# One task and one PSUM bank for each head's scores, and a finer end, in a kernel of attention and a gated mixer

## The chip, the cores and the metric

The kernel runs on one core of a Trainium2 chip. The metric is the device time of one execution in microseconds, lower is better. "Profile" and "trace" mean one execution taken by the hardware profiler; its lines give engine, source line (L1601 is line 1601 of the kernel), operation and shapes.

## The reference

Two branches work on the same normalised input of 2048 rows and 640 columns. Branch A is attention with 32 heads of 20 columns, branch B a mixer that shifts columns along the sequence and a two-layer MLP. The output is x + A * silu(B).

```python
def _A_ref(x, wqkv, wo):          # B, S, D = 1, 2048, 640; H = 32; Dh = 20
    q, k, v = ...                 # from x @ wqkv, per head
    scores = jnp.einsum("bhqd,bhkd->bhqk", q, k) * (Dh ** -0.5)
    p = _softmax(scores, axis=-1)
    o = jnp.einsum("bhqk,bhkd->bhqd", p, v)
    return (...o as rows...) @ wo

def _B_ref(x, w1, w2, w3, w4):
    h = _gelu(_layernorm(x, axis=-1) @ w1)
    # four column groups of h, shifted by +1, -1, +2, -2 rows
    hs = jnp.concatenate([g0, g1, g2, g3], axis=-1) @ w2
    x1 = x + hs
    return x1 + _gelu(_layernorm(x1, axis=-1) @ w3) @ w4

xn = _layernorm(x, axis=-1)
return x + _A_ref(xn, A_wqkv, A_wo) * _silu(_B_ref(xn, B_w1, B_w2, B_w3, B_w4))
```

## The kernel before

The work of attention is cut into 8 quads of four heads (`attn_quad`, L1356), each into four chunks of 512 queries, and each chunk into 16 tiles of 128 keys. For a key tile, TensorE makes scores of 128 keys by 512 queries for each of the four heads; then the exponentials are taken, and TensorE multiplies them by the values and sums over the 16 key tiles in PSUM bank 7 (L1414, L1592).

One head's scores of a key tile fill one PSUM bank (512 float32 in each partition). Banks 0 to 6 are a pool from which all products take their space. The kernel works on scores two heads at a time: a *pair* is heads 0 and 1 (a = 0) or heads 2 and 3 (a = 1) of one key tile, and it lies in two banks side by side. An exponential covers such a pair, 128 x 1024 elements. Most are taken by ScalarE (`exp_act`, L1658, the ACTIVATE of L1663). For the key tiles that `order` marks as blocks (`score_both`, L1669), one of the two pairs goes to VectorE instead, which makes the exponent's bits as 16-bit integers in U (L1694); VectorE and GpSimd then add constants (L1580, L1578), and four products with the values follow (L1592). Thirteen key tiles are "wide": all four heads in four banks and one ScalarE instruction (`score_rows`, L1629; L1645).

Scores come in two forms. In the *row form* (L1601) a head's 32 partitions of keys and queries use one strip of 32 rows of the array, and the four heads' strips can work side by side. In the *column form* (L1616) the query matrix QM holds zeros for the other heads, all 128 rows are used, and a head takes four matmuls that lie side by side in strips of 32 columns. Everything else on TensorE uses strips of columns: the helper `mm_tile` (products at L715: projections, the mixer, the output projection) and the products with the values.

`score_pair` (L1603) is the task that makes one pair: it gets its two banks together (`acq=("S", hs)`), waits until both are free, issues two row matmuls (or eight column matmuls), and increments TensorE's semaphore after the last. `AGAIN` in the configuration names pairs that are computed twice, ten of them in quad 7.

Nothing loops on the device. The program builds a list of tasks with their reads and writes; `TABLE`, a long string at the end of the file, gives the order in which they are taken, with the banks that each gets. `Planner.follow` (L219) reads it, works out which scores take the row form (a task marked `flex` does so if it stands next to another one of scores), and `plan_sync` (L323) puts a semaphore wait ahead of a task for each task of another engine that it needs and that isn't known to be done. Each engine then runs its own list strictly in that order. A task marked `lock` is one on VectorE that isn't to meet GpSimd's work.

The end of the kernel is the last chunk (quad 7, chunk 3), cut in two halves of 256 queries (`last_half`, L1426). A half is normalised by four VectorE steps: transpose (L1545), reciprocal (L1547), multiply (L1552), transpose (L1554). Then follow, for each of its two output tiles of 128 rows, the product with the last quad's rows of wo (`wo_last`, L1831; matmuls L1840), a VectorE instruction that reads the product from PSUM and multiplies by the gate (L1847), and in `finish_qc` (L1866) an addition (L1890) and the store (L1892). Stores of even and odd tiles have a semaphore each (`stream=f"out{sl}"`), and a store waits until the one before it of the same name has landed.

Of the kernel before, what the change touches and what calls it, by code (L numbers as in the profile page):

```python
# [57 lines left out]
class Planner:  # L58
# [89 lines left out]
    def task(self, eng, dur, fn, reads=(), writes=(), due=None, name="", lat=0.0,  # L148
# [8 lines left out]
        t.part = part or 3 * mode  # L157
# [61 lines left out]
    def follow(self, table):  # L219
# [26 lines left out]
        while at < len(table):  # L246
# [11 lines left out]
            if e == "pe" and pe_mode and t.mode:  # L258
                st = max(row_at + 6.0, *(row_end[x] for x in (1, 2) if t.part & x))
# [27 lines left out]
            if e == "pe":  # L287
                if t.mode != pe_mode:
                    t.finish += self.mode_cost
                if t.mode:  # L290
                    row_at = t.finish - t.dur
                    if not pe_mode:
                        row_end[1] = row_end[2] = 0.0
                    for x in (1, 2):
                        if t.part & x:
                            row_end[x] = t.finish
# [168 lines left out]
class Handle:  # L465
    _n = 0

    def __init__(self):
        Handle._n += 1
        self.id = Handle._n  # L470
        self.slot = None


class Cfg:
# [5 lines left out]
    def __init__(self, S=2048, D=640, H=32, F=1536):  # L480
# [100 lines left out]
        self.AGAIN = {(7, 0, 8, 1): 1, (7, 1, 1, 0): 1, (7, 1, 4, 0): 1, (7, 1, 5, 0): 1, (7, 1, 6, 0): 1, (7, 1, 7, 0): 1, (7, 1, 7, 1): 1, (7, 1, 9, 0): 1, (7, 1, 11, 0): 1, (7, 2, 15, 0): 1}  # L581
# [63 lines left out]
class Gen:  # L645
# [48 lines left out]

    def wtile(self):
# [26 lines left out]
    def build(self, plan_only=False):  # L722
        nc, pl = self.nc, self.pl
        with contextlib.ExitStack() as es:
# [13 lines left out]
            pl.kind("S2", "B", [(2 * (k > 1), p) for k, p in enumerate(pairs)] + [(3, [i, j]) for i in range(7) for j in range(i + 2, 7)])  # L738
# [617 lines left out]
    def attn_quad(self, quad):  # L1356
# [9 lines left out]
        for qc in range(NQC):  # L1366
# [21 lines left out]
            for kind, x, *unit in seq:  # L1388
# [12 lines left out]
                else:  # L1401
# [4 lines left out]
                    slots = (self.score_both(b, qc, ka, 0, quad, r, gb if col else None), self.score_both(b, qc, kb, 1, quad, r, gb if col else None))  # L1406
                    blocks.append((x, (kb, ka)))
                    if r == n - 1:
                        self.block_bits(quad, qc, blocks, ends)
                def fnpv(e, kts=kts, slots=slots, ends=ends):  # L1410
                    pb = self.bank(PVB)
                    first, final = ends()
                    for i in range(4):
                        ins = e.matmul(pb[32 * i:32 * i + 22, 0:512], VA[:, ql, kts[i // 2], i, :],  # L1414
                                       PT[:, slots[i // 2][0].slot, 512 * (i % 2):512 * (i % 2) + 512],
# [10 lines left out]
    def last_half(self, quad, qc, half, gb):  # L1426
# [35 lines left out]
        def pair(kk, a, kind):  # L1462
            hs, sa = self.stile()
            me = []
            def fn(e):
                for m, kt in enumerate(kk):
                    for jj in range(2):
# [11 lines left out]
                        name=f"sh{half}_{kk[0]}{kind}{a}", cls=-1, acq=("S", hs), flex=True, part=a + 1))  # L1479
# [6 lines left out]
        for x, kt in enumerate(ks):  # L1486
# [16 lines left out]
            for unit in at.get(x, []) + (at.get(x + 1, []) if cfg.HP else []):  # L1503
# [3 lines left out]
                for m, kx in enumerate(unit):  # L1507
                    hs, sa = pair(unit, m, "d") if cfg.HP else scores(kx, "d")
                    T("dve", c_dve(1024),
                      lambda e, m=m, hs=hs, ub=ub: e.tensor_scalar(U[:, ub, 1024 * m:1024 * m + 1024], self.psum[:, 512 * hs.slot:512 * hs.slot + 1024],  # L1510
# [31 lines left out]
        OnT = self.On[:, 0, c0:c0 + 256]  # L1542
# [6 lines left out]
        def fnn(e):  # L1549
            r = RZ[:, 0, h8:h8 + 8]  # L1550
            in1 = bass.AP(r.tensor, r.offset, [list(r.ap[0]), [1, 8], [0, 32]])
            return e.tensor_tensor(OnT.rearrange("p (a b) -> p a b", b=32), Ob[:, c0:c0 + 256].rearrange("p (a b) -> p a b", b=32), in1, op=ALU.mult)  # L1552
        T("dve", c_dve(256, "1x"), fnn, reads=[ob(0), ob(1)], writes=[ob(2)] + ([A("On", 0)] if half == 0 else []), name=f"onT_h{half}", cls=cls, lock=True)
        T("dve", c_dve(256, "1x"), lambda e: e.transpose(self.On7[:, 512 * qc + c0:512 * qc + c0 + 256], OnT), reads=[ob(2)],  # L1554
          writes=[A("On7", 2 * qc + half)], name=f"on_h{half}", cls=cls)

    def block_bits(self, quad, qc, blocks, ends):
# [10 lines left out]
        for v in range(4):  # L1568
# [16 lines left out]
            for n, (j, kts) in enumerate([] if acc and v == 0 else blocks):  # L1585
                def fn(e, v=v, dst=dst, n=n, j=j, kts=kts):
                    pb = self.bank(self.PVB)
                    first, final = ends()
                    for i in range(4):
                        at = 2048 * n + 512 * i  # L1590
# [12 lines left out]
    def score_pair(self, b, qc, kt, a, hs, sa, gb):  # L1603
        T, A = self.T, self.A
        me = []
        quad = int(self.tag.split("_")[0])
        early = self.tag == "0_0" and kt < self.cfg.EARLY
        times = 1 + self.cfg.AGAIN.get((quad, qc, kt, a), 0)
        def fn(e):
            for jj in list(range(2)) * times:  # L1610
                out = self.bank(hs[jj].slot if isinstance(hs, tuple) else hs.slots[jj])
                if me[0].mode:
                    ins = self.score(e, out[:, :], b, qc, kt, 2 * a + jj, early)
                    continue
                for c in range(4):
# [623 lines left out]
```

## Time and profile before

| | us |
|---|---|
| three runs | 793.1, 792.95, 793.8 |
| median of the runs | 793.1 |
| the profiled execution's own time | 792.01 |
| its span, from the first to the last instruction | 790.3 |
| ScalarE busy | 760.0 |
| VectorE busy | 705.3 |
| GpSimd busy | 441.2 |

How to read its lines: PE is TensorE's matmuls and PEld its weight loads, ACT is ScalarE, DVE VectorE, POOL GpSimd, SPq the queue of the engine that issues DMAs. A group line has the source line, engine, operation, what is written and read with its shapes, and the count; after the first bar the busy time and the mean in ns of one instruction; after the second the idle time of the engine just before them and what ended most of it. A waits line has who waited for whom, the total in us, how many times, and the longest. A timeline line has start and duration in us, and merges instructions of the same line that follow one another. A source line has the least, median and largest duration in ns. A windows line gives each engine's busy time in a stretch, with the count of its instructions. Matmul ends are modelled, so TensorE's rate is better read from the distance between starts.

### The profile page before, as it was taken

Reading aid. Unit: us, or ns where it says so; the run is one execution under the profiler, and the core shown is the slowest. Engines: PE = TensorE matmul, PEld = TensorE weight load, DVE = VectorE, ACT = ScalarE, POOL = GpSimd, SP = SyncE. Lnnn points to the kernel's source line nnn. Section 1 sums busy time; section 2 is a strip of 40 time slices with the busy share of each in tenths; the row PEclk is TensorE's granted clock in tenths of the full one; section 3 lists DMA queues with packets and bytes.
Section 4 is the critical chain, followed back from the end, with each engine's and each line's share of the span. In section 5 each row is a group of like instructions: output and inputs, shape, how many; then the busy total and the mean of one; then the engine's idle time right before and its main releaser. Section 6 shows DMA issues by size and latency. Waiting matters only on the chain.

```text
span 790.3 us, 29581 instructions
## 1 busy us (share of the span) xinstructions
PE 773.1 (98%) x13382; PEld 320.8 (41%) x13382; DVE 705.3 (89%) x934; ACT 760.0 (96%) x790; POOL 441.2 (56%) x238
## 2 busy tenths in 40 slices
PE   9999999999999999999999999999999999999996
PEld 5433333334444333333534444333334343333554
DVE  8898889889899999988998889898989899897986
ACT  7999999999999999999999999999999999999895
POOL 5667556562646647565654664765643645536742
PEclk9999999999999999999999999999999999999999
DMA  6422443332032322433243142333240114114343
GB/s 175 79 66 72 112 98 95 81 92 59 17 75 45 61 62 66 79 71 82 63 83 68 34 77 55 67 72 62 65 113 20 37 34 96 20 20 123 104 137 111
DMA packets 141357, 58.22 MB, mean 74 GB/s; under 512 B 113728, under 2 KB 136432, under 8 KB 141232
## 3 DMA queue, kind: packets, MB, share of 16 engines
q1 hardware_dynamic: 141232, 56.33, 31.1%
q8 instruction: 105, 1.72, 0.9%
q14 instruction: 20, 0.16, 0.1%
HBM read 34.70 MB, written 10.33 MB: 57 GB/s over the span
## 4 chain that ended last, share of the span: by engine, by line
PE 62%; ACT 35%; DVE 2%; DMA 1%; issue 0%; DVEq 0%
ACT arena L1663 30%; PE psum L715 22%; PE psum L1601 14%; PE psum L1592 10%; PE psum L1414 7%; PE psum L1616 6%; PE psum L889 1%; ACT arena L2074 1%; ACT arena L1645 1%; ACT arena L1982 1%; DVE arena L1694 1%; PE psum L1471 1%; ACT arena L2102 1%; DMA arena<-in_B_w_dram 1%; PE psum L1445 0%; PE psum L1061 0%
## 5 line engine op out<-in xcount | busy, mean ns | idle before, releaser
L1663 ACT ACTIVATE arena<-psum 128x1024 bf16<-128x1024 f32 x718 | 671.5, 1036 | 16.9 <-PE psum L1601 11.5
L1578 POOL TENSOR_TENSOR arena<-arena 128x2048 int32<-128x2048 int32 x92 | 330.2, 3600 | 199.9 <-DVE arena L1580 105.4
L1694 DVE TENSOR_SCALAR arena<-psum 128x1024 uint16<-128x1024 f32 x276 | 335.3, 1219 | 46.9 <-PE psum L1601 43.3
L715 PE MATMUL psum<-arena 128*32 128x320 bf16 (+1 forms) x5808 | 332.8, 332 | 1.0 <-DMA arena<-in_B_w_dram 0.8
L1601 PE MATMUL psum<-arena 32*128 32x512 bf16 x1644 | 199.3, 384 | 7.0 <-ACT arena L1663 3.5
L715 PEld LDWEIGHTS psum<-arena 128*32 128x32 bf16 x5808 | 143.6, 96 | 122.2 <-issue 32.4
L1592 PE MATMUL psum<-arena 128*22 128x512 bf16 x2208 | 187.6, 381 | 0.1
L1580 DVE TENSOR_SCALAR arena<-arena 128x4096 uint16<-128x4096 uint16 (+1 forms) x139 | 142.2, 1041 | 3.6 <-PE psum L1592 2.9
L1414 PE MATMUL psum<-arena 128*22 128x512 bf16 x1432 | 136.0, 381 | 0.3 <-ACT arena L1663 0.2
L1601 PEld LDWEIGHTS psum<-arena 32*128 32x128 bf16 x1644 | 54.8, 91 | 176.1 <-ACT arena L1663 91.1
L1616 PE MATMUL psum<-arena 128*32 128x512 bf16 x1440 | 109.5, 380 | 0.3
L1729 POOL TENSOR_TENSOR arena<-arena 128x512 bf16<-128x512 f32 x30 | 41.2, 1372 | 70.9 <-DVE arena L1580 36.5
L1592 PEld LDWEIGHTS psum<-arena 128*22 128x22 bf16 x2208 | 51.6, 91 | 61.1 <-issue 28.7
L1414 PEld LDWEIGHTS psum<-arena 128*22 128x22 bf16 x1432 | 35.5, 91 | 48.8 <-issue 20.9
L1616 PEld LDWEIGHTS psum<-arena 128*32 128x32 bf16 x1440 | 30.2, 95 | 36.8 <-ACT arena L1663 26.3
L2067 DVE CAST arena<-psum 128x512 bf16<-128x512 f32 x48 | 32.8, 686 | 3.2 <-PE psum L715 2.7
L1281 DVE CAST arena<-psum 128x512 bf16<-128x512 f32 x40 | 27.0, 682 | 5.1 <-PE psum L715 4.6
L1890 POOL TENSOR_TENSOR arena<-arena 128x640 bf16<-128x640 bf16 x12 | 16.6, 1401 | 21.2 <-DVE arena L1521 10.2
L926 DVE BATCH_NORM_STATS2 arena<-arena 128x6 f32<-128x320 bf16 x54 | 24.5, 478 | 1.6 <-DMA arena<-in_A_x_dram 1.6
L1645 ACT ACTIVATE arena<-psum 128x2048 bf16<-128x2048 f32 x13 | 24.6, 1891 | 0.7 <-PE psum L1601 0.7
L1716 DVE STREAM_TRANSPOSE arena<-psum 128x512 f32<-128x512 f32 x30 | 21.3, 710 | 2.7 <-PE psum L1592 1.6
L1828 DVE SCALAR_TENSOR_TENSOR arena<-psum,arena 128x320 bf16<-128x320 f32 x32 | 15.0, 488 | 7.5 <-PE psum L715 7.3
(133 smaller groups left out, 343.6 us busy)
## 6 DMA issues: line engine op xcount, KB each, us to landing
arena<-in_B_w_dram SPq DMA_DIRECT2D x48, 160.0 KB, 2.8
arena<-arena SPq DMA_DIRECT2D x124, 32.0 KB, 1.9
arena<-in_B_w_dram SPq DMA_DIRECT2D x4, 960.0 KB, 6.0
arena<-in_A_x_dram SPq DMA_DIRECT2D x8, 320.0 KB, 5.4
arena<-in_A_x_dram SPq DMA_DIRECT2D x16, 160.0 KB, 2.4
out_dram<-arena SPq DMA_DIRECT2D x16, 160.0 KB, 2.5
heads<-arena SPq DMA_DIRECT2D x120, 20.0 KB, 2.0
arena<-queries SPq DMA_DIRECT2D x28, 80.0 KB
```

What stands on the lines that cost most here:

```text
L715: ins = e.matmul(pb[32 * c:32 * c + 32, 0:N], lhsT(k, c), rhs(k, c), start=(k == 0), stop=(stop and k == nk - 1), tile_position=(0, 32 * c))
L1414: ins = e.matmul(pb[32 * i:32 * i + 22, 0:512], VA[:, ql, kts[i // 2], i, :], PT[:, slots[i // 2][0].slot, 512 * (i % 2):512 * (i % 2) + 512],
L1578: return e.tensor_tensor(dst.bitcast(I32), U[:, ub, 0:w].bitcast(I32), bass.AP(c.tensor, c.offset, [list(c.ap[0]), [0, w // 2]]), op=ALU.add)
L1580: fa if onp else lambda e, v=v, dst=dst: e.tensor_scalar(dst, U[:, ub, 0:w], EXP_B[v], None, op0=ALU.add),
L1592: ins = e.matmul(pb[32 * i:32 * i + 22, 0:512], wv, dst[:, at:at + 512].bitcast(BF16), start=first, stop=final, tile_position=(0, 32 * i))
L1601: return e.matmul(out, self.KT[32 * i:32 * i + 32, b, 128 * kt:128 * kt + 128], q, start=True, stop=True, tile_position=(32 * i, 0))
L1616: ins = e.matmul(out[32 * c:32 * c + 32, :], self.KT[:, b, 128 * kt + 32 * c:128 * kt + 32 * c + 32], self.QM[:, gb, 2 * a + jj, :], start ...
L1645: lambda e: e.activation(self.PT[:, hp[0].slot:hp[0].slot + 2, :], self.psum[:, 512 * h0.slot:512 * h0.slot + 2048].rearrange("p (a b) -> ...
L1663: lambda e: e.activation(self.PT[:, hp.slot, :], self.psum[:, 512 * hs.slot:512 * hs.slot + 1024], AF.Exp, scale=cfg.scale),
L1694: ins = e.tensor_scalar(U[:, ub, 1024 * at + 512 * k:1024 * at + 512 * k + w], self.psum[:, 512 * hd.slots[k]:512 * hd.slots[k] + w], a_ex ...
L1729: return e.tensor_tensor(OnT.rearrange("p (k d a) -> p a k d", k=4, a=4), Ob[:, :].rearrange("p (a k d) -> p a k d", a=4, k=4), in1, op=AL ...
L2067: T("dve", c_dve(512), lambda e, h=h, fc=fc, i=i, G=G: e.tensor_copy(G[:, i, fc, :], self.wbank(h)[:, 0:512]), reads=[wa], writes=at, name ...
```

## The change

It has these parts:

- `score_pair` makes two tasks, one for each head. Each takes one bank (a new kind "S1": any one of the seven) and has its own waits and its own increment. The two banks of a pair still have to adjoin, in either order (`banks`, `Handle.at`); the exponential reads both tasks' results. The repeats of `AGAIN` are now counted for each head.
- The planner knows four row strips instead of two.
- ScalarE's and VectorE's reads of a pair are written as two banks of 512 elements. The version of `score_both` that split VectorE's instruction, which the configuration had switched off, is gone.
- The second half of the last chunk is multiplied and transposed in two parts of 128 queries; tile 14 needs the first part, tile 15 the second.
- For tile 15, ScalarE copies the product from PSUM (times 0.5), and VectorE multiplies by the gate from SBUF. Its store has a stream of its own.
- `TABLE` holds a new order of all tasks.

```diff
-            st = max(row_at + 6.0, *(row_end[x] for x in (1, 2) if t.part & x))
+            st = max(row_at + 4.0, *(row_end[x] for x in range(4) if t.part >> x & 1))
...
+    def at(self, k):
+        return 512 * (k ^ (self.two is not None and self.two[0].slot > self.two[1].slot))
...
-        self.AGAIN = {(7, 0, 8, 1): 1, (7, 1, 1, 0): 1, (7, 1, 4, 0): 1, (7, 1, 5, 0): 1, (7, 1, 6, 0): 1, (7, 1, 7, 0): 1, (7, 1, 7, 1): 1, (7, 1, 9, 0): 1, (7, 1, 11, 0): 1, (7, 2, 15, 0): 1}
+        self.AGAIN = {(2, 2, 4, 2): 2, (7, 0, 1, 0): 1, (7, 0, 1, 1): 1, (7, 0, 8, 2): 2, (7, 1, 5, 0): 1, (7, 1, 6, 2): 1, (7, 1, 7, 3): 1, (7, 1, 9, 0): 1, (7, 1, 12, 0): 1}
...
+    def banks(self, hs, n=512):
+        lo, hi = sorted(h.slot for h in hs) if isinstance(hs, tuple) else hs.slots
+        assert hi == lo + 1
+        p = self.psum[:, 512 * lo:512 * lo + n]
+        return bass.AP(p.tensor, p.offset, [list(p.ap[0]), [512 * (hi - lo), 2], [1, n]])
...
+            pl.kind("S1", "B", [(0, [i]) for i in range(7)])
...
-        def fnn(e):
-            r = RZ[:, 0, h8:h8 + 8]
...
-        T("dve", c_dve(256, "1x"), fnn, reads=[ob(0), ob(1)], writes=[ob(2)] + ([A("On", 0)] if half == 0 else []), name=f"onT_h{half}", cls=cls, lock=True)
-        T("dve", c_dve(256, "1x"), lambda e: e.transpose(self.On7[:, 512 * qc + c0:512 * qc + c0 + 256], OnT), reads=[ob(2)],
+        w = 256 >> half
+        for x in range(1 + half):
+            a = c0 + w * x
...
+            T("dve", c_dve(w, "1x"), fnn, reads=[ob(0), ob(1)], writes=[A("Obh", 2, half, x)] + ([A("On", 0)] if half == 0 else []),
+              name=f"onT_h{half}" + "y" * x, cls=cls, lock=True)
+            T("dve", c_dve(w, "1x"), lambda e, a=a, OnT=OnT: e.transpose(self.On7[:, 512 * qc + a:512 * qc + a + w], OnT), reads=[A("Obh", 2, half, x)],
+              writes=[A("On7", 2 * qc + half) if x == 0 else A("On7", 2 * qc + half, x)], name=f"on_h{half}" + "y" * x, cls=cls)
...
-        times = 1 + self.cfg.AGAIN.get((quad, qc, kt, a), 0)
-        def fn(e):
-            for jj in list(range(2)) * times:
...
-                    acq=("S2",) + hs if isinstance(hs, tuple) else ("S", hs)))
+        for jj, (h, sa) in enumerate(tiles):
+            i = 2 * a + jj
+            times = 1 + self.cfg.AGAIN.get((quad, qc, kt, i), 0)
+            me = []
+            def fn(e, h=h, i=i, me=me, times=times):
+                out = self.bank(h.slot)
+                for _ in range(times):
+                    if me[0].mode:
+                        ins = self.score(e, out[:, :], b, qc, kt, i, early)
+                        continue
...
+                        writes=[sa], name=f"sc{self.tag}_{kt}_{a}" + "y" * jj, mode=int(gb is None), part=1 << i, flex=gb is not None, cls=-1, times=times,
+                        acq=("S1", h)))
...
-               lambda e: e.activation(self.PT[:, hp.slot, :], self.psum[:, 512 * hs.slot:512 * hs.slot + 1024], AF.Exp, scale=cfg.scale),
+               lambda e: e.activation(self.PT[:, hp.slot, :].rearrange("p (a b) -> p a b", b=512), self.banks(hs), AF.Exp, scale=cfg.scale),
...
+            return e.tensor_scalar(U[:, ub, 1024 * at:1024 * at + 1024].rearrange("p (a b) -> p a b", b=512), self.banks(hd), a_exp, EXP_BIAS,
+                                   op0=ALU.mult, op1=ALU.add)
...
-        T("dve", c_dve(2 * HALF), fe, reads=[sa, A("xn", n)], writes=dsta, name=f"wobev{n}", rel=hs)
+        if n == self.cfg.NT - 1:
+            T("act", c_act(2 * HALF), lambda e: e.activation(half(dst), self.banks(hs, HALF), AF.Copy, scale=0.5), reads=[sa], writes=dsta,
+              name=f"wobac{n}", rel=hs)
+            T("dve", c_dve(2 * HALF, "2x"), lambda e: e.tensor_tensor(dst, dst, G[:, n, :], op=ALU.mult), reads=dsta + [A("xn", n)], writes=dsta,
+              name=f"wobev{n}", lock=True)
+            return
+        T("dve", c_dve(2 * HALF), lambda e: e.scalar_tensor_tensor(half(dst), self.banks(hs, HALF), 0.5, half(G[:, n, :]), op0=ALU.mult, op1=ALU.mult),
+          reads=[sa, A("xn", n)], writes=dsta, name=f"wobev{n}", rel=hs)
...
-              reads=resa, writes=[("out", n)], is_dma=True, nbytes=128 * cfg.D * 2, name=f"st_out{n}", stream=f"out{sl}",
+              reads=resa, writes=[("out", n)], is_dma=True, nbytes=128 * cfg.D * 2, name=f"st_out{n}", stream=f"out{sl}" if n < self.cfg.NT - 1 else "out2",
```

More of the change, by code (lines that the diff above doesn't have):

```diff
@@ L292, in follow @@
                     if not pe_mode:
[L293 to L295 removed]
+                        row_end[:] = [0.0] * 4
+                    for x in range(4):
+                        if t.part >> x & 1:
                             row_end[x] = t.finish
@@ L1656, in stile, with exp_two @@
         return h, a
+    def exp_two(self, tiles, tag):
+        hp, pa = self.exp_act(tuple(h for h, _ in tiles), [a for _, a in tiles], tag)
+        hp.two = tuple(h for h, _ in tiles)
+        return hp, pa
     def exp_act(self, hs, sa, tag):
```

285 lines of the change are left out of this document (142 added, 143 removed).

## The prediction

> **What bounds the kernel now.** I read first the busy shares and the chain of waits on the page, then the span cut into 40 us stretches, then who waited for whom, and last the timeline of TensorE and of the end.
>
> ```profile
> span 790.3 us, 29581 instructions
> PE 773.1 (98%) x13382; PEld 320.8 (41%) x13382; DVE 705.3 (89%) x934; ACT 760.0 (96%) x790; POOL 441.2 (56%) x238
> ...
> PE 62%; ACT 35%; DVE 2%; DMA 1%; issue 0%; DVEq 0%
> ```
>
> Two engines are full at once: TensorE (PE) 98%, ScalarE (ACT) 96%. The chain changes between them, so neither can be shortened far without the other.
>
> ```profile
> core 0: us, PE busy (x) PEld busy (x) DVE busy (x) ACT busy (x) POOL busy (x), PEclk, DMA share, GB/s
> 0.00:40.00 40.00, 38.04 (x840) 19.98 (x840) 32.89 (x104) 34.15 (x54) 24.94 (x52) 1.00 0.51 126
> ...
> 640.00:680.00 40.00, 39.35 (x656) 15.81 (x644) 35.66 (x40) 37.54 (x41) 24.24 (x8) 1.00 0.31 64
> ...
> 720.00:760.00 40.00, 39.41 (x790) 19.64 (x792) 34.94 (x51) 37.09 (x38) 20.82 (x11) 1.00 0.44 124
> 760.00:791.00 31.00, 23.72 (x644) 14.88 (x632) 22.39 (x40) 21.11 (x23) 11.12 (x8) 0.96 0.41 129
> sum 791.00, PE 773.08 PEld 320.77 DVE 705.27 ACT 760.05 POOL 441.19; mean PE 38.65 PEld 16.04 DVE 35.26 ACT 38.00 POOL 22.06
> ```
>
> Without the first 40 us and the last 31 us, 720 us remain. In them ACT is busy 760.05 - 34.15 - 21.11 = 704.8 us and idle 15.2; PE is busy 773.08 - 38.04 - 23.72 = 711.3 and idle 8.7. These two numbers bound what another order can win in the middle: about 15 us if ACT never waited again. The stretches at 640 and 720 alone hold 2.5 + 2.9 of ACT's idle time.
>
> ```profile
> ACT arena L1663 <- PE psum L1601: 11.5, 28, 1.2
> ...
> PE psum L1601 <- ACT arena L1663: 3.5, 14, 0.4
> ```
> ```profile
> L1663 ACT ACTIVATE arena<-psum 128x1024 bf16<-128x1024 f32 x718 | 671.5, 1036 | 16.9 <-PE psum L1601 11.5 <-PE psum L1471 2.4 <-PE psum L1414 0.8
> L1694 DVE TENSOR_SCALAR arena<-psum 128x1024 uint16<-128x1024 f32 x276 | 335.3, 1219 | 46.9 <-PE psum L1601 43.3
> ...
> L1601 PE MATMUL psum<-arena 32*128 32x512 bf16 x1644 | 199.3, 384 | 7.0 <-ACT arena L1663 3.5 <-DVE arena L1694 0.8 <-ACT arena L1645 0.6
> ...
> L1616 PE MATMUL psum<-arena 128*32 128x512 bf16 x1440 | 109.5, 380 | 0.3
> ```
>
> The wait that matters is ACT's for scores: 11.5 us in 28 waits ended by L1601. The score matmuls come in two shapes. L1601 gives one head per matmul and puts up to four heads side by side (row form); L1616 needs four matmuls for a head, so its 1440 are 360 heads (column form). How the two forms and the changes between them are paid for is seen in PE's timeline:
>
> ```profile
> 21.54 0.40 PE L1601 MATMUL psum<-arena 32*128 32x512 bf16 x4
> ...
> 561.58 0.39 PE L1414 MATMUL psum<-arena 128*22 128x512 bf16 x4
> 561.90 0.60 PE L1601 MATMUL psum<-arena 32*128 32x512 bf16 x4
> ...
> 562.66 0.39 PE L1592 MATMUL psum<-arena 128*22 128x512 bf16 x4
> 562.88 0.39 PE L715 MATMUL psum<-arena 128*32 128x512 bf16 x4
> ...
> 569.90 0.39 PE L1601 MATMUL psum<-arena 32*128 32x512 bf16 x4
> 570.23 0.40 PE L715 MATMUL psum<-arena 128*32 128x512 bf16 x4
> ...
> 701.82 0.39 PE L1601 MATMUL psum<-arena 32*128 32x512 bf16 x4
> 702.15 0.46 PE L715 MATMUL psum<-arena 128*32 128x320 bf16 x8
> ...
> 756.58 0.40 PE L1601 MATMUL psum<-arena 32*128 32x512 bf16 x4
> ```
>
> Column work follows column work 0.22 us later (562.66 to 562.88). Into the row form it takes 0.32 (561.58 to 561.90), out of it 0.33 (569.90 to 570.23): a change costs about 0.10 one way and 0.11 the other. From the first to the last row above I count 372 runs of L1601 between other work; 272 hold four heads and 84 hold six. So PE spends some 372 x 0.21 = 78 us on changing form. A full group of four heads costs one step of 0.22, and a late pair costs a step of its own: at 561.90 four heads take 0.60 instead of 0.39.
>
> **The change part by part.**
> *Score tasks.* The arithmetic stays: the same exponentials go to ACT (718) and DVE (276), which bound the time as before, so nothing is gained by volume. A score task is now one head with one bank instead of two heads with two neighbouring banks. A head may start when its own bank is free, a lone head may stand in column form without a change of form, and heads of different tasks can fill a group. The gain has to come out of the 11.5 us. Lower end: none of it, because both banks of a pair are freed by the same instruction wherever the pair was also read as a pair. Upper end: all 11.5. I take 4.0, nearest to what two rows allow: about a third of the waits, if every third pair straddles two earlier pairs; or one saved step of 0.22 in some 18 of the 84 runs with six heads. What hides the rest is PE itself, 98% busy: a score that comes earlier pushes other matmuls back, and those are late next for DVE (43.3 us of waits on L1601, off the path as long as U is in time). A loss is possible as well; it is priced as a rival.
>
> *Repeated scores.* Before, ten pairs are computed twice: 10 extra steps of 0.22 = 2.2 us. After, nine heads have 11 repeats; each repeat of a head uses the same rows again and so needs a step: 11 x 0.22 = 2.4 us at most. Bounds -2.2 and +2.4; I take 0, as they lie mostly in quad 7 beside ACT's waits (the stretch at 720). Without that cover they would cost the difference, 0.2.
>
> *Operands in two pieces.* The reads of L1663 and L1694 are now written as two banks of 512. The banks still adjoin, and L1847, which reads two pieces of 320, takes 818 ns against 488 for one piece of L1828 (rows below): 1.03 ns a column, and by the same slope L1694 would take 488 + 704 x 1.03 = 1213 of its measured 1219. So a second piece costs nothing; I take 0. If it cost 0.01 us on each of the 718 exponentials, that would be 7.2 us on ACT with no cover. I see no row for a gain.
>
> *The end.*
>
> ```profile
> 783.90 0.20 DVE L1547 RECIPROCAL arena<-arena 128x8 f32<-128x8 f32 x1
> 784.14 0.42 DVE L1552 TENSOR_TENSOR arena<-arena 128x256 bf16<-128x256 f32 x1
> 784.60 0.45 DVE L1554 STREAM_TRANSPOSE arena<-arena 128x256 bf16<-128x256 bf16 x1
> 785.10 0.39 PEld L1840 LDWEIGHTS psum<-arena 128*32 128x32 bf16 x16 [2.20 <-DVE arena L1554]
> ...
> 785.61 1.56 DVE L1847 SCALAR_TENSOR_TENSOR arena<-psum,arena 128x640 bf16<-128x640 f32 x2 [0.56 <-PE psum L1840]
> 787.08 0.88 DVE L1890 TENSOR_TENSOR arena<-arena 128x640 bf16<-128x640 bf16 x2
> ```
> ```profile
> L1645 ACT ACTIVATE arena<-psum 128x2048 bf16<-128x2048 f32 x13 | 24.6, 1891 | 0.7 <-PE psum L1601 0.7
> ...
> L1828 DVE SCALAR_TENSOR_TENSOR arena<-psum,arena 128x320 bf16<-128x320 f32 x32 | 15.0, 488 | 7.5 <-PE psum L715 7.3
> ...
> L1663 ACT ACT_TABLE_LOAD x3 | 3.8, 1283 | 0.1
> ...
> L1847 DVE SCALAR_TENSOR_TENSOR arena<-psum,arena 128x640 bf16<-128x640 f32 x4 | 3.2, 818 | 1.1 <-PE psum L1840 1.1
> ```
> ```profile
> L1069 ACT ACTIVATE arena<-psum x9: 591/598/637, 11.6 to 27.2; 128x512 bf16<-128x512 bf16 x9
> ```
> ```profile
> out_dram<-arena SPq DMA_DIRECT2D x7, 160.0 KB, 2.3
> ```
>
> Half the width saves 128 x 1.03 = 0.13 on each of the two first steps: multiply 784.14 to 784.43, transpose (0.04 later) 784.47 to 784.79. Tile 14 starts on PE 0.05 later, at 784.84, and could be read 0.51 after that (785.10 to 785.61), at 785.35. In between DVE does the second multiply and transpose, 0.29 + 0.32 and a gap, until about 785.42; then it reads tile 14, 785.45 to 786.27. Tile 15 is on PE at 785.47 and can be read at 785.98; ACT has nothing left to do and copies it. The nearest row is a copy of 512 columns, 0.60; with 128 columns more at the 1.03 of DVE it is 0.73, so 786.71. DVE meanwhile adds tile 14 (0.48) to 786.77, then multiplies tile 15 (the same form as the add, 0.48) and adds it: 787.25, 787.77. Before it was 787.08 + 0.88 = 787.96: gain 0.2. One end is 0.8, if tile 15's read left the path altogether; the other a loss of 1.1, if the copy needed a table load (1.28 us on ACT). The nine copies of L1069, at 11.6 to 27.2 us, share that time with the first exponentials (scores start at 21.5), and no table load stands on L1069's line, so I take the gain. The last store gets a queue of its own; the store before it lands some 2.3 us after its issue, which is just before the new issue at 787.8, so this keeps the gain and adds none: 0 (up to 0.2 lost without it).
>
> *Sum.* 792.0 us is the profiled execution's own time, 1.7 around its span of 790.3. 792.0 - 4.0 + 0 + 0 - 0.2 = 787.8. The median of the runs, 793.1, is 1.1 above that execution, so on the median: 793.1 - 4.2 = **788.9 us**, its own range 786 to 791.4.
>
> **The rivals.**
> *More than that:* the finer tasks remove nearly all of ACT's waits for scores. For it speaks that these waits are only 28 and that PE has 8.7 us idle in the middle; against it that PE's idle time is in splinters. 793.1 - 11.5 - 0.2 = 781.4.
>
> *Only the end is faster:* both banks of a pair come free together, so a single head never starts sooner. For it: 272 of 372 runs are full groups of four already. 793.1 - 0.2 = 792.9.
>
> *Slower by split groups:* heads placed one by one break up groups in PE's queue; one run turned into two costs two changes, 0.21, and one more step, 0.22, together 0.43 us. It decides once it eats PE's idle 8.7 us: from 20 more runs on each adds in full to the time. For it: every head now has a wait of its own in a queue that is executed in order, and behind it stand the matmuls of the values (L1414, L1592) that free ACT's tiles. One run in twelve split, 31 of 372: 31 x 0.43 - 8.7 = 4.6 later, less 0.2: 797.5.
>
> *Slower by increments:* each head now increments a semaphore, where a pair did it once. 1644 less 13 x 4 of the wide tiles (L1645, row above) are 796 pairs, so 796 more. The run at 701.82 is such a wide tile with one increment for four heads, the one at 569.90 has two, and both leave the row form after 0.33 us. So one increment costs less than the 0.01 that the rows resolve, 796 x 0.01 = 8.0 us at most, which PE's idle 8.7 would hold; if it held none: 793.1 + 8.0 - 0.2 = 800.9. The Trainium skill ("TensorE: Matmul & The Clock Gate", "The cost: per-tile semaphore tail") speaks against the change here: increments of concurrent tiles serialise, 26.3 ns for each one more. By that rule, if the tail lay in PE's way, 796 x 26.3 ns would be an estimated 21 us more. The equal 0.33 of the two rows does not show it.
>
> **How the numbers follow.** Chances: the forecast 0.57, more than that 0.14, only the end 0.11, split groups 0.15, increments 0.03. The predicted time is the likeliest case's, 788.9. The range 783 to 797 takes in the forecast, the case of the end alone, the weaker half of the larger gain and most of the split groups, and leaves out the far ends. A measurement of this kernel can tell about 0.2% (1.6 us) from no change: faster means below 791.5, slower above 794.7. Faster is 0.57 + 0.14 = 0.71; the same is 0.11; slower is 0.18.
>
> **What would show it.** In the changed profile: ACT's waits for the row form fall from 11.5 to about 7 us; ACT's idle time between 40 and 760 us falls from 15.2 to about 11; PE's busy time falls by some 4 us with no more than 372 runs of the row form; means of 1036 and 1219 ns stay; from the last reciprocal's start to the end of the last add is 3.9 us instead of 4.1, and no table load stands before the copy. It is wrong if the runs of the row form grow by more than 20, if the exponential's mean grows, or if ACT's idle time in the middle stays.

## The result, and the profile after

| | before | after |
|---|---|---|
| median of 14 runs each, same chip | 792.88 us (791.41 to 793.93) | 791.29 us (790.55 to 791.99) |
| ratio, 95% interval | | 0.998 [0.9972, 0.9989] |
| profiled execution: its own time, its span | 792.0, 790.3 us | 791.3, 789.6 us |

The change makes the kernel faster by 1.6 us (0.9 to 2.2 by the interval); the forecast was 4.2. The page of the changed kernel, in the order of the first part of the prediction. L1615 is now the row form of the scores, L1632 the column form, L1684 the exponential on ACT, L1707 the one on DVE.

```profile
span 789.6 us, 27717 instructions
PE 774.8 (98%) x12461; PEld 294.0 (37%) x12461; DVE 704.1 (89%) x936; ACT 760.5 (96%) x791; POOL 441.7 (56%) x238
...
PE 67%; ACT 26%; DVE 6%; issue 0%
...
L1684 ACT ACTIVATE arena<-psum 128x1024 bf16<-128x1024 f32 x718 | 671.6, 1041 | 17.0 <-PE psum L1615 12.6
...
L1707 DVE TENSOR_SCALAR arena<-psum 128x1024 uint16<-128x1024 f32 x276 | 335.6, 1221 | 47.9 <-PE psum L1615 44.4
...
L1615 PE MATMUL psum<-arena 32*128 32x512 bf16 x1935 | 257.7, 384 | 6.5 <-ACT arena L1684 2.7
...
L1632 PE MATMUL psum<-arena 128*32 128x512 bf16 x240 | 23.4, 381 | 0.1
```

The column form has almost gone: 240 matmuls, 60 heads, where before there were 1440 for 360 heads. PE's busy time rose from 773.1 to 774.8 instead of falling by 4. The waits of the changed kernel (total us, count, longest):

```profile
ACT arena L1684 <- PE psum L1615: 12.6, 30, 0.8
...
PE psum L1615 <- ACT arena L1684: 2.7, 9, 0.5
```

ACT's waits for scores did not fall to 7 either: 12.6 us in 30 waits after 11.5 in 28. The stretches (columns as before):

```profile
0.00:40.00 40.00, 38.14 (x834) 19.97 (x838) 33.19 (x104) 33.38 (x54) 24.11 (x52) 1.00 0.45 109
40.00:760.00 720.00, 713.00 (x11019) 259.49 (x11007) 648.09 (x791) 705.44 (x715) 405.98 (x179) 1.00 0.31 69
```

ACT's idle time in the middle is 720 - 705.4 = 14.6 us (15.2 before; about 11 was forecast). Only the end came as worked out. Its timeline (start, duration):

```profile
783.58 0.20 DVE L1556 RECIPROCAL arena<-arena 128x8 f32<-128x8 f32 x1
783.81 0.49 DVE L1565 TENSOR_TENSOR arena<-arena 128x128 bf16<-128x128 f32 x2
784.22 0.50 DVE L1568 STREAM_TRANSPOSE arena<-arena 128x128 bf16<-128x128 bf16 x2
...
784.58 0.73 PE L1852 MATMUL psum<-arena 128*32 128x320 bf16 x16 [1.55 <-DVE arena L1568]
784.65 0.45 DVE L1906 TENSOR_TENSOR arena<-arena 128x640 bf16<-128x640 bf16 x1
785.09 0.83 DVE L1863 SCALAR_TENSOR_TENSOR arena<-psum,arena 128x640 bf16<-128x640 f32 x1
...
785.36 0.70 ACT L1858 ACTIVATE arena<-psum 128x640 bf16<-128x640 f32 x1 [2.77 <-PE psum L1852]
785.95 0.49 DVE L1906 TENSOR_TENSOR arena<-arena 128x640 bf16<-128x640 bf16 x1
786.36 0.49 DVE L1860 TENSOR_TENSOR arena<-arena 128x640 bf16<-128x640 bf16 x1
786.88 0.49 DVE L1906 TENSOR_TENSOR arena<-arena 128x640 bf16<-128x640 bf16 x1
```

From the reciprocal's start to the end of the last add: 786.88 + 0.49 - 783.58 = 3.79 us, before 787.96 - 783.90 = 4.06. The gain is 0.27 (0.2 forecast). To the last instruction of the trace the distance falls from 6.39 to 6.03 us, by 0.36. ACT's copy takes 0.70 (0.73 estimated) and no table load stands before it.

### The profile page after: what moved, and what is told of

Read it like the earlier page. It is cut to its first block, busy times and chain, and to the rows that moved or that the text cites. A ratio compares the mean times of both kernels' runs of the same rounds, so it can differ in the third digit from the quotient of the medians.

```text
span 789.6 us, 27717 instructions
## 1 busy us (share of the span) xinstructions
PE 774.8 (98%) x12461; PEld 294.0 (37%) x12461; DVE 704.1 (89%) x936; ACT 760.5 (96%) x791; POOL 441.7 (56%) x238
## 4 chain that ended last, share of the span: by engine, by line
PE 67%; ACT 26%; DVE 6%; issue 0%
PE psum L725 23%; ACT arena L1684 22%; PE psum L1615 19%; PE psum L1606 12%; PE psum L1424 8%; DVE arena L1707 3%; PE psum L899 1%; ACT arena L2090 1%; PE psum L1632 1%; ACT arena L1998 1%; PE psum L1481 1%; ACT arena L1661 1%; ACT arena L2118 1%; DVE arena L1594 1%; PE psum L1455 1%; PE psum L1071 0%
## 5 line engine op out<-in xcount | busy, mean ns | idle before, releaser
L1684 ACT ACTIVATE arena<-psum 128x1024 bf16<-128x1024 f32 x718 | 671.6, 1041 | 17.0 <-PE psum L1615 12.6
L1707 DVE TENSOR_SCALAR arena<-psum 128x1024 uint16<-128x1024 f32 x276 | 335.6, 1221 | 47.9 <-PE psum L1615 44.4
L1615 PE MATMUL psum<-arena 32*128 32x512 bf16 x1935 | 257.7, 384 | 6.5 <-ACT arena L1684 2.7
L1606 PE MATMUL psum<-arena 128*22 128x512 bf16 x2208 | 193.0, 381 | 0.3 <-DVE arena L1594 0.3
L725 PEld LDWEIGHTS psum<-arena 128*32 128x32 bf16 x5808 | 137.4, 96 | 120.4 <-issue 50.6
L1615 PEld LDWEIGHTS psum<-arena 32*128 32x128 bf16 x1935 | 69.2, 91 | 227.8 <-ACT arena L1684 133.4
L1424 PE MATMUL psum<-arena 128*22 128x512 bf16 x1432 | 135.2, 382 | 0.0
L1606 PEld LDWEIGHTS psum<-arena 128*22 128x22 bf16 x2208 | 49.5, 90 | 65.8 <-issue 43.7
L1424 PEld LDWEIGHTS psum<-arena 128*22 128x22 bf16 x1432 | 34.0, 90 | 49.2 <-issue 28.6
L953 POOL TENSOR_SCALAR arena<-arena 128x640 bf16<-128x640 bf16 x16 | 13.9, 875 | 19.2 <-DVE arena L1594 14.2
L1632 PE MATMUL psum<-arena 128*32 128x512 bf16 x240 | 23.4, 381 | 0.1
```

Of the source, the lines that this page charges most:

```text
L725: ins = e.matmul(pb[32 * c:32 * c + 32, 0:N], lhsT(k, c), rhs(k, c), start=(k == 0), stop=(stop and k == nk - 1), tile_position=(0, 32 * c))
L1606: ins = e.matmul(pb[32 * i:32 * i + 22, 0:512], wv, dst[:, at:at + 512].bitcast(BF16), start=first, stop=final, tile_position=(0, 32 * i))
L1615: return e.matmul(out, self.KT[32 * i:32 * i + 32, b, 128 * kt:128 * kt + 128], q, start=True, stop=True, tile_position=(32 * i, 0))
L1632: ins = e.matmul(out[32 * c:32 * c + 32, :], self.KT[:, b, 128 * kt + 32 * c:128 * kt + 32 * c + 32], self.QM[:, gb, i, :], start=True, st ...
L1684: lambda e: e.activation(self.PT[:, hp.slot, :].rearrange("p (a b) -> p a b", b=512), self.banks(hs), AF.Exp, scale=cfg.scale),
L1707: return e.tensor_scalar(U[:, ub, 1024 * at:1024 * at + 1024].rearrange("p (a b) -> p a b", b=512), self.banks(hd), a_exp, EXP_BIAS, op0=A ...
```

## The experiments

Two things had to be explained: the time, and the runs of the row form, which the forecast capped at 372. A run is a stretch of row-form matmuls with no other matmul between them. Taken run by run from PE's matmuls over the whole trace there are 382 before and 566 after, and 186 of the 566 hold just two heads. The cause is a rule in `follow` that the change left as it was: a `flex` task takes the row form if it stands next to another such task. Before, a lone pair was one task and stood in column form; now it is two tasks, one beside the other, and takes the row form.

So the readings to tell apart were: the 180 or so extra runs eat the gain (two changes of form each); the row form is itself the gain; the increments eat the gain (TensorE's planned increments rose from 3442 to 4408, 966 more, one for each pair); the finer tasks never had a gain, and the end is all. Letters in the expectations are short names of such readings. Every kernel below ran in five rounds beside the kernel before on its chip; "before" had medians of 792.09, 792.07 and 792.10 us in the three sets, and 0.001 of a ratio is 0.79 us. The ratio is not the quotient of the two medians; the two differ by up to 0.0007.

| kernel | us | ratio to before [95%] |
|---|---|---|
| before + new end | 791.27 | 0.9991 [0.9982, 0.9999] |
| after, old end | 791.84 | 0.9995 [0.9987, 1.0004] |
| after, lone pairs in column form | 793.65 | 1.0022 [1.0013, 1.0031] |
| before, lone pairs in row form | 791.78 | 0.9997 [0.9988, 1.0007] |
| **after, one increment a pair** | **787.70** | **0.9949 [0.9936, 0.9961]** |
| before, head tasks | 794.44 | 1.0027 [1.0015, 1.0038] |
| before, head tasks, one increment a pair | 791.92 | 0.9996 [0.9987, 1.0005] |
| after, pair tasks | 792.39 | 1.0005 [0.9996, 1.0013] |
| after, needed increments only | 787.79 | 0.9940 [0.9928, 0.9952] |
| before, needed increments only | 792.27 | 0.9999 [0.9990, 1.0007] |
| after, one increment, lone pairs in column form | 791.26 | 0.9987 [0.9978, 0.9995] |
| after, one increment, no repeats | 788.21 | 0.9944 [0.9932, 0.9956] |

**The end alone, and all but the end.** The first kernel is the old one with the new `onT`, `wobac15` and store at the end; the second is the new one with the old end.

```diff
-        T("dve", c_dve(256, "1x"), fnn, ..., name=f"onT_h{half}", cls=cls, lock=True)
+        w = 256 >> half
+        for x in range(1 + half):
...
+        if n == self.cfg.NT - 1:
+            T("act", c_act(2 * HALF), lambda e: e.activation(half(dst), self.banks(hs, HALF), AF.Copy, scale=0.5), ...
```

> The kernel before with only the new end: last half multiplied and transposed in two parts, the addition of tile 13 moved behind them, ScalarE's copy for tile 15, its own stream. Theory A (the end gives 0.3 to 0.6 us of the 1.6, the score tasks and the order give the rest): 0.3 to 0.6 us faster than before, ratio 0.9993 to 0.9996. Theory B (the end is the whole gain): 1.6 us faster, ratio 0.998. From the last reciprocal's start to the last addition's end both expect 3.8 us instead of 4.1.

> The changed kernel with the old end (256 queries in one part, VectorE reads tile 15, tile 13 added first). Theory A: 1.0 to 1.3 us faster than before, ratio 0.9984 to 0.9987. Theory B: no faster than before, ratio 1.000.

Measured: the end alone gains 0.7 us (0.1 to 1.4). The changed kernel with the old end stands at 0.9995 against 0.998 with the new one, 1.2 us apart. Both intervals are as wide as the effect; they agree with the timelines to within their width. From the last reciprocal to the last instruction the traces of the two kernels with the old end have 6.39 us each, those of the two with the new end 6.02 and 6.03. By the timelines the end is about a quarter of the 1.6 us; the runs would allow half. All the rest of the change together, as it was made, is then worth about 0.4 us, with no change inside its interval.

**The extra runs of the row form.** A lone pair is put back into column form; `run` is the number of heads of scores that stand together on PE.

```diff
-                if t.flex and (pe_mode or (nx is not None and (nx.mode or nx.flex))):
+                if t.flex and run[t.id] > 2:
```

> The changed kernel, same order, but a run of scores with only one pair in it takes the column form, as before; that brings the runs of the row form from 566 back to 388. Theory C (the 184 more changes of form eat the gain that the finer tasks make): 2 to 3 us faster than the changed kernel, ratio to before about 0.995, and ACT's waits for scores below 11 us. Theory D (a lone pair costs TensorE the same 0.43 us in either form, so the number of runs doesn't matter): as the changed kernel, ratio 0.998.

And the reverse in the kernel before: every flex pair takes the row form.

```diff
-                if t.flex and (pe_mode or (nx is not None and (nx.mode or nx.flex))):
+                if t.flex and (t.name[:2] == "sc" or pe_mode or (nx is not None and (nx.mode or nx.flex))):
```

> The kernel before, same order, but the 180 lone pairs take the row form; its runs rise from 382 to 562. Theory G (TensorE pays 0.43 us for a lone pair either way, but in the row form both heads start 0.10 us after the work before them, in the column form the second starts 0.22 after, so the exponential may begin 0.1 us earlier): about 3 us faster than before, ratio 0.995 to 0.997. If the row form only paid in the changed order, because that was made for it: ratio 1.000 or slower.

The first has 388 runs and loses 3.3 us against the changed kernel (1.0022 to 0.998); the second has 562 and stays where it was. So 180 more runs cost nothing measurable in the one order, and are worth 3.3 us in the other. The extra runs did not eat the gain; nor does the row form bring one by itself.

**The increments.** Where a task of another engine needs both heads of a pair, it now waits for the later one alone, which PE does last in any case. The earlier head has then no one who needs its count and does not increment. Nothing else is touched: the same order, forms and banks.

```diff
+        for t in tasks:
+            heads = [p for p in t.preds if tasks[p].name[:2] == "sc"]
+            if t.eng != "pe" and len(heads) > 1:
+                for p in sorted(heads, key=lambda p: tasks[p].pos)[:-1]:
+                    t.preds.discard(p)
+                    tasks[p].succs.remove((t.id, True))
         for t in tasks:
             t.signals = any(sync for (_, sync) in t.succs)
```

> The changed kernel, same order and forms, but only the later head of a pair increments TensorE's semaphore; 966 increments fewer (3442 instead of 4408), as many as before. If increments cost what the rival of the prediction gave at most (0.01 us each), up to 8 us faster than the changed kernel, ratio to before 0.988; if they cost nothing in this stream: as the changed kernel, ratio 0.998.

787.7 us, ratio 0.9949: 0.0031 of the ratio, 2.5 us, faster than the changed kernel, and 4.0 faster than before, which is about what the forecast wanted of the whole. The widths of the two intervals leave about 1.3 to 3.7 us for the 2.5; the two profiled spans, 789.6 and 786.0, are 3.6 apart. The same was then asked in the old order: the code of the changed kernel with the order, forms and end of the old one, each pair of `TABLE` written as two heads one after the other, with all 4408 increments and with 3442. In outline:

```diff
-    sc..._a        [two banks]
+    sc..._a        [first bank]
+    sc..._ay       [second bank]
```

> The kernel before (its order, banks, forms, repeats and end) with each pair's score task split into two consecutive head tasks: 4408 increments instead of 3442, nothing else. Theory E (each increment more lands about 30 ns after the one before it and so holds up the exponential that waits for the later head): about 3 us slower than before, ratio 1.003 to 1.005. Theory F (the increments only cost in the changed order): ratio 1.000.

> The same split of the kernel before, but only the later head of a pair increments: waits for each head's bank stay, the increments are 3442 again. Theory E: as before, ratio 1.000. If separate tasks and waits cost something by themselves: slower than before, as e5.

Splitting with all increments costs 2.1 us against before (1.0027), without them nothing (0.9996): 0.0031, 2.5 us, once more, and the spans (793.2 and 789.6) are again 3.6 apart. The separate tasks and their own waits are in both kernels, so they are not the cause. The page's row of ACT's exponentials in the four kernels, the changed one's shown above; columns are busy us, mean ns, idle us before them. First the changed kernel with one increment a pair:

```profile
L1690 ACT ACTIVATE arena<-psum 128x1024 bf16<-128x1024 f32 x718 | 669.6, 1046 | 15.7 <-PE psum L1621 11.9 <-PE psum L1487 1.3 <-PE psum L1430 1.3
```

Then the old order with head tasks, all increments:

```profile
L1690 ACT ACTIVATE arena<-psum 128x1024 bf16<-128x1024 f32 x718 | 673.0, 1034 | 18.3 <-PE psum L1621 12.7 <-PE psum L1491 2.3 <-PE psum L1434 0.9
```

And the same with one increment a pair:

```profile
L1696 ACT ACTIVATE arena<-psum 128x1024 bf16<-128x1024 f32 x718 | 671.3, 1036 | 16.6 <-PE psum L1627 11.3 <-PE psum L1497 2.3 <-PE psum L1440 0.8
```

Busy and idle have to be added here, since an exponential that follows at once overlaps the one before it, which lengthens its mean and shortens the sum. (In the trace of the kernel before, 646 of the 718 start while another instruction of ACT is still running, by 0.12 us in the mean; they last 1037 ns in the mean, the 72 others 1024.) The sums are 669.6 + 15.7 = 685.3 against 671.6 + 17.0 = 688.6 in the new order, 687.9 against 691.3 in the old one. The increments cost ACT 3.3 and 3.4 us. The waits for scores alone (12.6 to 11.9) show little of it.

Where it happens can be seen at one place in the two traces of the new order, a full group of four heads for which ACT stands waiting. With all increments:

```profile
740.78 0.40 PE L1615 MATMUL psum<-arena 32*128 32x512 bf16 x4
741.11 0.86 PE L725 MATMUL psum<-arena 128*32 128x320 bf16 x20
741.27 1.02 ACT L1684 ACTIVATE arena<-psum 128x1024 bf16<-128x1024 f32 x1 [0.56 <-PE psum L1615]
```

With one a pair:

```profile
737.38 0.40 PE L1621 MATMUL psum<-arena 32*128 32x512 bf16 x4
737.70 0.86 PE L731 MATMUL psum<-arena 128*32 128x320 bf16 x20
737.81 1.02 ACT L1690 ACTIVATE arena<-psum 128x1024 bf16<-128x1024 f32 x1 [0.51 <-PE psum L1621]
```

PE goes on at the same time in both: the next matmul comes 0.33 and 0.32 after the group. (Over the traces of before, after and this kernel, the median of groups of four that PE leaves without waiting is 325 ns with one increment, with two and with four.) ACT starts 0.49 after the group in the one and 0.43 in the other. The semaphore events of the trace say why. A wave is the row matmuls that start together, in fact some 3 ns one after the other. From the start of a head's own matmul to its step of PE's semaphore, medians in ns:

```
heads that increment in one wave      lands after
before:                    1          404
                           2          404  440
after:                     2          399  430
                           3          399  429  460
                           4          399  430  460  491
after, one a pair:         1          403
                           2          406  439   (waves of four heads)
```

The heads of a wave start within 10 ns, but their increments land one by one, 34 ns apart. Of these 3 are the distance of the starts, so each increment comes some 30 ns later than the one before it. The last head of a full group is known to be done at 491 instead of 440, the second of a lone pair at 430 instead of 404. The Trainium skill ("TensorE: Matmul & The Clock Gate", "The cost: per-tile semaphore tail") says that increments of concurrent tiles serialise at 26.3 ns each; the 30 ns here are near it, a little more.

How such steps add up can be seen by lining up the two traces of the new order at the starts of their 566 runs of the row form. The distance between them grows by 3.3 us from the first run to the last, and not at one place:

```
growth from one run to the next   times   sum, us
under 20 ns either way            458     0.24
20 to 40 ns                        57     1.51
40 to 60 ns                        33     1.63
over 60 ns                          2     0.40
-20 ns and below                   15    -0.50
```

Ninety places of 20 to 60 ns make 3.14 us. At most of the others the distance hardly changes. The two kernels in the old order show the same: 77 such steps of 381, 2.58 us. In the new order much of it can be seen coming back to PE inside the runs: at 84 scores that wait for another engine the distance from the matmul before is 15 ns or more longer than in the faster kernel, at 46 of them behind VectorE (1.6 us), at 35 behind ScalarE (1.1 us) and at three behind both; 25 such scores give 0.9 us back. That fits engines that learn late of the last head and so hand their banks back late, VectorE as much as ScalarE.

**Are increments dear by themselves?** Here every increment was dropped whose count no wait refers to. Most of those dropped belong to tasks that do not share their moment with another head.

```diff
+        for t in tasks:
+            if t.signals and not t.is_dma and t.seq not in used[t.eng]:
+                t.signals = False
```

> The changed kernel, but only those tasks increment a semaphore to whose count some wait refers: on TensorE 1393 increments instead of 4408 (and 191 fewer on VectorE, 59 on GpSimd, 27 on ScalarE). Order and forms stay. If each increment in a group that nobody waits for delays the ones behind it, as the kernel with one increment a pair suggests (3442 left, 787.7 us), then of a full group of four heads only one lands where two did: another 30 ns or so sooner for the waiting engine, and the time falls further, to 784 to 787. If what mattered was only the second increment of a pair, 787.7 again, within 0.7. If TensorE lost time to increments as such, its busy time falls well below the 771.0 us of the kernel with one increment a pair.

> The kernel before, with needed increments alone: 1385 on TensorE instead of 3442. The same question in the other order. If increments nobody waits for delay those behind them: 1 to 3 us faster than before, ratio 0.996 to 0.999. If only the split of a pair's increment cost time: no change, ratio 0.9993 to 1.0007.

Nothing clear of the noise, in either order: 787.79 us here and 787.70 with one increment a pair (0.9940 and 0.9949, each of its own set), and 0.9999 against before. The first of the two leaves the tasks' needs as they were and drops the increments alone, so the gain of one increment a pair does not hang on how it was brought about. The expectation that a full group would go down to one increment was wrong for most: of 254 waves of four heads 185 still have two, at 405 and 439, since both their pairs are waited for. What was dropped were some 2050 increments elsewhere on PE, and by the second kernel's interval, 0.8 us at most, one of them costs less than 0.0004 us. It is not their number, it is several at one moment with a waiter behind the last.

**Does the gain need finer tasks, and the row form?** In the first of these kernels the new order has pair tasks (one increment each, both banks at the place of the later head; lone pairs in the row form, 609 runs); in the second, tasks are heads with one increment a pair, and lone pairs are in column form.

```diff
-                        acq=("S1", h)))
+                    writes=[sa for _, sa in tiles], ..., acq=[("S1", h) for h, _ in tiles]))
```

> The changed kernel's order with each pair made by one task again, at the place of its later head, all pairs in the row form, one increment: the finer tasks undone, the order kept (609 runs of the row form instead of 566). If starting a head before its pair's other bank is free is worth something: slower than the changed kernel with one increment a pair (ratio 0.995), by 1 us or more. If not: 0.995 as well.

> The changed kernel with one increment a pair, and the pairs that stand alone between other work in column form again (about 388 runs of the row form instead of 566). With all increments the column form cost 3.3 us in this order. If it costs them because of how the column form serves the engines that wait (its second head starts 0.22 after its first), it costs the same here: 790.5 to 791.5. If the increments were part of that (four increments instead of two on a way that is longer), it costs less than half of it: 788 to 789.3.

Against 0.9949, pair tasks lose 4.4 us (1.0005) and the column form 3.0 (0.9987; 3.7 against the 0.9940 of its own set). The loss by the column form is as large as with all increments, so the increments have no part in it. PE's row on the page of the second one:

```profile
PE 775.1 (98%) x13538; PEld 321.3 (41%) x13538; DVE 703.4 (89%) x936; ACT 761.6 (96%) x791; POOL 441.9 (56%) x238
```

and of the kernel with one increment a pair and the row form:

```profile
PE 771.0 (98%) x12461; PEld 293.4 (37%) x12461; DVE 702.7 (89%) x936; ACT 758.5 (97%) x791; POOL 441.2 (56%) x238
```

PE is busy 4.1 us less with 178 more runs of the row form, 0.023 us for each lone pair. By itself that says little, since PE is busy for 98% of either span and the spans differ by 3.8 us. Taken at the lone pairs themselves, the distance from the step before to the step after has a median of 639 ns in row form and 648 in column form (means 620 and 644). The prediction's rows say the same to within their rounding: two heads in column form are 2 x 0.22 = 0.44, one row step with two changes 0.22 + 0.21 = 0.43. In the old order the medians are 639 and 647, and PE's busy time fell as well, from 773.1 us, with lone pairs in row form:

```profile
PE 770.7 (98%) x12302; PEld 291.9 (37%) x12302; DVE 705.4 (89%) x934; ACT 759.0 (96%) x790; POOL 441.3 (56%) x238
```

But the time did not follow. Why one order can use it and the other cannot was not settled.

**The repeats.**

```diff
-        self.AGAIN = {(2, 2, ...
+        self.AGAIN = {}
```

> The changed kernel with one increment a pair and without the 11 repeated scores (the list of repeats is empty). The forecast put them at 0, bounds +2.4 and -2.2. If they are hidden: 787.7 again, within 0.7. If they stand in TensorE's way: 785.3 to 787. If they stop a wait or hold the order together: 788.5 to 790.

788.21 beside the 787.79 of its own set, 0.9944 beside 0.9940: no difference clear of the noise, which is some 1.3 us between two such ratios.

## Why the prediction was right in its direction and wrong in its size

*Score tasks, 4.0 us.* With the increments set aside the whole change is worth 4.0 us by the ratio, of which the end has 0.3 to 1: 3 to 3.7 us are left, near the 4.0. The way there was another one, so that the size came out near is luck. The tasks as such, in the old order, gain nothing (0.9996); the new order with pair tasks gains nothing (1.0005); with head tasks and lone pairs in column form it gains what the end may account for (0.9987). In the new order both head tasks and the row form are needed; the old order with both of them and one increment a pair was not run. ACT's listed waits for scores, out of which the prediction wanted the gain, stayed at 11.9 us even in the fastest kernel. The gain shows in ACT's exponentials, busy and idle together (688.4 before, 685.3). PE's 771.0 us is no sign of it: the old order with lone pairs in row form has 770.7 and gains nothing. As a sign of the gain the wait total was badly chosen.

*A lone head in column form.* "A lone head may stand in column form without a change of form" went the other way: heads leave the column form, and the runs of the row form grew by 184 where 20 were to be the sign of a loss. The rival of split groups fails: its 0.43 us for an extra run is the price of a full group torn in two, and the runs of four heads hardly changed, 272 before and 267 after. Each extra run replaces two column steps, which cost as much (639 against 648 ns).

*Increments: the step that failed.* The sum has no term for them. The prediction said that one increment costs less than 0.01 us, since the runs at 701.82 and 569.90, with one increment and two, both leave the row form after 0.33. That is true and it is still so with four. But the row shows when PE goes on, and the price is paid by the engine that waits for the last head: 30 ns for each increment ahead of its own, at some 90 places, 2.5 us by the ratios and 3.3 by the two traces lined up. The rows that could have told it were ACT's starts after a group it was waiting for, or the semaphore events of the kernel before, 404 and 440. The count was off too: 796 leaves out the 180 pairs in column form and counts the ten repeats, and 966 were added. The rival named the right cause with the wrong mechanism and gave it 0.03; as "8.0 us at most, which PE's idle 8.7 would hold" it looked for the cost on the engine that does not pay it. The estimate of 21 us by the Trainium skill's rule was put under the condition that the tail lies in PE's way; it does not, so the size per increment nearly held and the sum did not.

*Repeats* at 0: nothing against it, within 1.3 us. *Operands in two pieces* at 0: the old order with head tasks and one increment reads every operand as two banks and takes 0.9996, with the same mean of 1036. In the changed kernel the mean grew to 1041, which the prediction had called a sign that it was wrong; it is a sign of more overlap (0.115 us before, 0.120, and 0.127 in the fastest kernel, whose mean is 1046). *The end* at 0.2: 0.27 to 0.36 by the timeline; the runs, 0.7 and 1.2, can't separate it from more.

The sum that would have been right: 4.0 gained by order, heads, row form and end together, 2.5 given back by the increments, 1.5 left; measured 1.6. The 2.5 has to be that of the old order here, which was measured apart; that of the new order is the difference between the 4.0 and the 1.6 itself. That 791.29 lies just inside the forecast's own 786 to 791.4 bears out none of its terms.

## What to carry to other kernels

When matmuls run side by side, let only the last one that somebody waits for increment the semaphore. Here that one edit, in the same order, turns 0.998 into 0.9949, better than both kernels. And price an increment where it is waited for: the row to look up is the start of the waiting engine after it, not the next start of the engine that sends it. Small costs that repeat at many hand-overs are found by lining up two traces by the same events and looking at the steps between them.

## What the runs showed of the hardware that was not expected

Increments of concurrent row-form matmuls land 399, 430, 460 and 491 ns after the start of each one's own matmul (399, 433, 467 and 501 after the first start), while PE leaves the form after the same 325 ns with one, two or four. Increments that nobody waits for, most of them alone at their moment, are free within the measurement (2057 fewer on PE: 0.9999 [0.9990, 1.0007]). And a pair of heads that stands alone is no dearer in row form, with its two changes, than in column form without them: 639 against 648 ns from the step before to the step after.
